# A Fourier mixing and SoLU kernel: the first stage reordered, weight conversion between the folds

## The chip, the cores and the metric

The kernel runs on one core of one Trainium2 chip. The metric is the device time of one execution in microseconds; lower is better. Before the change it was 1299.51 us, the median of three runs (1297.58 to 1300.37).

## The reference

```python
X = np.fft.fft(np.fft.fft(x, axis=1), axis=2).real   # x: (8, 3136, 256)
h = X.reshape(25088, 256) @ w_in                     # w_in: (256, 1024)
e = np.exp(h - h.max(-1, keepdims=True))
solu = h * e / (e.sum(-1, keepdims=True) + 1e-9)
ln = (solu - mean(solu)) / sqrt(var(solu) + 1e-6) * g_ln
out = ln @ w_out                                     # w_out: (1024, 256)
```

The weights arrive as 64-bit floats, x as 32-bit floats; all work is done in 32 bits.

## The kernel before, in words

**The transform.** The sequence of 3136 is split into 49 x 64. The eight sequences are taken in four pairs. For one pair x is read in eight chunks of four columns (`load`: a plain part xa on SP's queue, L98, and a mirrored part xb by an indirect transfer on GpSimd's queue, L100). `add_mirror` (L120, L121, GpSimd) adds the mirrored part, `fold` (L111 to L113, VectorE) folds the 256 features, `transform1` (L151, TensorE) does the 49-point transform of two columns, ScalarE copies the result to z (L154), and SP stores z to the DRAM buffer zd once per chunk (L156). The tiles xa and xb have two buffers, so chunk c + 2 is loaded when chunk c is folded. `turn` (L163, GpSimd's queue) reads zd back in another order, five frequencies at a time, as four transfers into a tile g; `transform2` (L174) does the 64-point transform of one frequency.

**The units.** 25 frequencies for each of four pairs make 100 units. A unit has up to two signs with 128 rows each. Its instructions: `up` (L200, TensorE, product with the prepared w_in), `even` and `join` (L206, L214, VectorE), `expo` (L225, ScalarE), `product` (L233, VectorE, and L235, GpSimd), `square` (L242, ScalarE), the turn of 32 x 32 blocks (L269, VectorE), the move of the turned blocks (L278, SP's queue, 16 transfers for two units), `stats` (L249 to L257, GpSimd). Four units later `down` (L284, TensorE) multiplies with the prepared w_out, ScalarE scales (L289) and the result is stored. While pair p is in its units, the chunks of pair p + 1 are loaded, summed, folded and transformed, one step per unit (`ahead` and `ahead_pe`).

**The first stage.** For pair 0 nothing can run beside the units, so its eight chunks go through `ahead` and `ahead_pe` alone. In the same time ScalarE's queue loads the tables and both weights. Then `prepare` runs: VectorE converts w_in from 64 to 32 bits (`narrow`, L316 to L347, four pieces of 512 columns), TensorE multiplies it with the feature table Q (L379), VectorE converts w_out (eight pieces of 256 columns), scales it by g_ln (L384), and subtracts its column mean (L388 to L391). The scratch pool of this stage is closed before the working pool of the units is opened in its place.

**What sets the order.** The schedule is written by hand: each engine carries out its instructions in the order of the program, and each waits for the data and the buffers it needs. A transfer is issued by the engine whose queue it stands in, in that order.

Of the kernel before, what the change touches and what calls it, by code (L numbers as in the profile page):

```python
# [33 lines left out]
def kernel(  # L34
# [272 lines left out]
    def load_weight(pool, w, o, engine):  # L307

        if w.dtype == FP32:
            engine.dma_start(out=o, in_=w.rearrange("(c p) f -> p c f", p=P))  # L310
            return lambda: None
        raw = pool.tile([P, o.shape[1], 2 * w.shape[1]], I32, name=f"raw_{w.tensor.name}")
        engine.dma_start(out=raw, in_=w.bitcast(I32).rearrange("(c p) f -> p c f", p=P))

        def bits(o, i, a, op0, b=None, op1=ALU.bypass):
            nc.vector.tensor_scalar(out=o, in0=i, scalar1=a, scalar2=b, op0=op0, op1=op1)  # L316

        n = min(w.shape[1], 512)

        def narrow(c, j):  # L320
            def tmp(name, dt=I32):
                return pool.tile([P, n], dt, tag=name, name=name)

            lo, hi = raw[:, c, 2 * j : 2 * (j + n) : 2], raw[:, c, 2 * j + 1 : 2 * (j + n) : 2]

            ex = tmp("ex")
            bits(ex, hi, 20, ALU.logical_shift_right, 0x7FF, ALU.bitwise_and)
            bits(ex, ex, -896.0, ALU.add, 0.0, ALU.max)
            bits(ex, ex, 255.0, ALU.min)
            bits(ex, ex, 23, ALU.logical_shift_left)  # L330

            unit = tmp("unit")
            bits(unit, hi, 31, ALU.logical_shift_right, 31, ALU.logical_shift_left)
            nc.vector.tensor_tensor(out=unit, in0=unit, in1=ex, op=ALU.bitwise_or)  # L334
            top = tmp("top")
            bits(top, hi, 0xFFFFF, ALU.bitwise_and, 3, ALU.logical_shift_left)
            nc.vector.tensor_tensor(out=top, in0=top, in1=unit, op=ALU.bitwise_or)

            half, rest = tmp("ex"), tmp("rest", FP32)
            bits(half, lo, 16, ALU.logical_shift_right, 0xFFFF, ALU.bitwise_and)  # L340
            bits(rest, half, 2.0 ** -36, ALU.mult)
            half = tmp("ex")
            bits(half, lo, 0xFFFF, ALU.bitwise_and)
            nc.vector.scalar_tensor_tensor(out=rest, in0=half, scalar=2.0 ** -52, in1=rest,  # L344
                                           op0=ALU.mult, op1=ALU.add)
            nc.vector.tensor_tensor(out=rest, in0=rest, in1=unit.bitcast(FP32), op=ALU.mult)  # L346
            nc.vector.tensor_tensor(out=o[:, c, j : j + n], in0=rest, in1=top.bitcast(FP32), op=ALU.add)  # L347
# [206 lines left out]
```

## Time and profile before

| | us |
|---|---|
| median of three runs | 1299.51 |
| the profiled execution | 1302.77 |
| its span, first to last instruction | 1301.0 |
| TensorE busy in the span | 1184.9 (91%) |
| VectorE busy | 959.6 (74%) |
| ScalarE busy | 610.2 (47%) |
| GpSimd busy | 554.1 (43%) |

The profile is one execution. Engines: PE is TensorE, PEld its weight loads, DVE is VectorE, ACT is ScalarE, POOL is GpSimd, SP is the engine that issues most transfers; a q behind a name is the engine's sequencer. Starts are in us from the first instruction of the span. In a row, "out<-in" gives the tiles, "x8" the number of instructions merged, and the part in brackets the idle time of the engine ahead of the row and what ended it. PEclk is the clock that TensorE was granted, as a share of 2.4 GHz.

### The profile page before, as it was taken

To read this page: it belongs to the slowest core of one execution; us is meant where nothing else is said; L and a number is where in the kernel's file an instruction comes from. 1 tells how busy PE (TensorE), PEld (TensorE's weight loads), DVE (VectorE), ACT (ScalarE), POOL (GpSimd) and SP (SyncE) were. 2 spreads that over 40 slices of the span, in tenths; PEclk is the share of its full clock that TensorE was granted. 3 is DMA by queue.
4 is the path that set the end of the run, shared out by engine and by line. 5 is a ranking of instruction groups with operands and counts; after the bars stand their busy time and mean duration, and the time that the engine had idled before them with its cause. 6 is when DMAs were issued, how large, how long until landed. Compare 5 with 4: busy or idle time off the path is not lost.

```text
span 1301.0 us, 15863 instructions
## 1 busy us (share of the span) xinstructions
PE 1184.9 (91%) x4864; PEld 899.4 (69%) x4864; DVE 959.6 (74%) x1481; ACT 610.2 (47%) x1149; POOL 554.1 (43%) x972
## 2 busy tenths in 40 slices
PE   1432679999999999999999999999999999999997
PEld 1210347777777777777777777787777777777786
DVE  2399788777777788787777788777777787777770
ACT  1100245545555455555555455555454555555551
POOL 2530245454445355554345445444454333333331
PEclk9656889999999999999999999999999999999999
DMA  9660067886579967665588769675598546454543
GB/s 232 216 152 0 27 132 167 169 164 160 136 146 179 174 149 188 151 165 140 136 172 171 182 146 178 154 169 145 130 172 165 125 111 145 102 133 103 136 106 100
DMA packets 464628, 189.53 MB, mean 146 GB/s; under 512 B 433206, under 2 KB 446782, under 8 KB 464288
## 3 DMA queue, kind: packets, MB, share of 16 engines
q1 hardware_dynamic: 444752, 144.45, 51.1%
q0 software_dynamic: 13824, 38.55, 11.4%
q10 hardware_dynamic: 5968, 5.52, 1.9%
q8 instruction: 40, 0.66, 0.2%
q14 instruction: 44, 0.36, 0.1%
HBM read 44.78 MB, written 38.80 MB: 64 GB/s over the span
## 4 chain that ended last, share of the span: by engine, by line
PE 86%; DVE 8%; DMA 3%; issue 1%; POOL 1%; ACT 0%; POOLq 0%; DVEq 0%; ACTq 0%
PE ps_o L284 52%; PE ps_h L200 25%; PE ps L151 4%; PE ps L174 3%; DMA xa<-in_x_dram 2%; DVE ex L316 2%; DMA xb<-in_x_dram,idx 1%; PE ps L176 1%; POOL xa L120 1%; DVE u L233 1%; DVE h L214 1%; DVE v L269 1%; DVE rest L344 0%; DVE rest L346 0%; DVE unit L334 0%
## 5 line engine op out<-in xcount | busy, mean ns | idle before, releaser
L284 PE MATMUL ps_o<-Wo,uT 128*128 128x256 f32 x3136 | 699.6, 381 | 2.7 <-DMA uT<-v 2.7
L284 PEld LDWEIGHTS ps_o<-Wo,uT 128*128 128x128 f32 x3136 | 613.3, 197 | 65.2 <-issue 3.5
L200 PE MATMUL ps_h<-Wi,q 128*128 128x512 f32 x800 | 363.3, 597 | 13.1 <-DVE ev L206 11.6
L233 DVE SCALAR_TENSOR_TENSOR u<-h,u 128x1024 f32<-128x1024 f32 x196 | 232.5, 1223 | 139.3 <-ACT u L225 139.3
L225 ACT ACTIVATE u<-h,neg 128x1024 f32<-128x1024 f32 x196 | 223.7, 1142 | 200.2 <-DVE neg L219 200.2
L235 POOL TENSOR_SCALAR nmean<-usum 128x1 f32<-128x1 f32 x196 | 127.7, 652 | 433.7 <-DVE u L233 433.4
L242 ACT ACTIVATE h<-u,nmean 128x1024 f32<-128x1024 f32 x196 | 223.6, 1142 | 124.4 <-POOL nmean L235 124.4
L214 DVE CUSTOM_DVE_ANT_0 h<-ev,ps_h 128x1024 f32<-128x1024 f32 x196 | 231.8, 1219 | 48.0 <-PE ps_h L200 44.4
L200 PEld LDWEIGHTS ps_h<-Wi,q 128*128 128x128 f32 x800 | 152.9, 192 | 163.2 <-issue 147.2
L269 DVE STREAM_TRANSPOSE v<-u 128x1024 f32<-128x1024 f32 x200 | 238.1, 1230 | 0.1
L206 DVE SCALAR_TENSOR_TENSOR ev<-w_mid,q,ps_h 128x1024 f32<-128x1024 f32 x100 | 127.6, 1276 | 61.8 <-PE ps_h L200 61.0
L182 ACT COPY q<-ps 128x257 f32<-128x257 f32 x100 | 37.3, 373 | 205.7 <-PE ps L176 203.8
L151 PE MATMUL ps<-y,F 98*100 98x258 f32 (+3 forms) x288 | 81.2, 422 | 47.0 <-DVE y L113 47.0
L296 POOL DMA_INDIRECT out_dram<-ot,idx x96 | 102.6, 1069 | 46.1 <-issue 21.9
L254 POOL TENSOR_SCALAR v<-ssq 128x2 f32<-128x2 f32 (+1 forms) x100 | 27.6, 276 | 170.1 <-ACT h L242 170.1
L289 ACT ACTIVATE ot<-ps_o,rs 128x256 f32<-128x256 f32 x196 | 80.8, 456 | 30.4 <-PE ps_o L284 30.4
L174 PEld LDWEIGHTS ps<-T,g 128*128 128x128 f32 x400 | 60.4, 191 | 47.4 <-issue 47.3
L151 PEld LDWEIGHTS ps<-y,F 98*100 98x100 f32 x288 | 48.4, 192 | 61.0 <-DVE y L113 26.9
L120 POOL TENSOR_TENSOR xa<-xa,xb 98x1020 f32<-98x1020 f32 (+1 forms) x32 | 72.7, 2273 | 29.7 <-DMA xa<-in_x_dram 19.7
L257 POOL TENSOR_TENSOR rs<-v,neg_half 128x2 f32<-128x2 f32 (+1 forms) x100 | 71.9, 719 | 7.8
L174 PE MATMUL ps<-T,g 128*128 128x128 f32 x400 | 60.8, 275 | 0.0
L163 POOL DMA_DIRECT2D g<-zd x80 | 47.5, 604 | 20.6 <-DMA zd<-z 11.3
(53 smaller groups left out, 491.6 us busy)
## 6 DMA issues: line engine op xcount, KB each, us to landing
uT<-v SPq DMA_DIRECT2D x784, 128.0 KB
zd<-z SPq DMA_DIRECT2D x32, 400.0 KB
g<-zd POOLq DMA_DIRECT2D x80, 160.0 KB, 5.3
out_dram<-ot SPq DMA_DIRECT2D x100, 128.0 KB
xa<-in_x_dram SPq DMA_DIRECT2D x32, 392.0 KB
raw_in_moe_w_in_dram<-in_moe_w_in_dram ACTq DMA_DIRECT2D x1, 2048.0 KB
raw_in_moe_w_out_dram<-in_moe_w_out_dram ACTq DMA_DIRECT2D x1, 2048.0 KB
uT<-v SPq DMA_DIRECT2D x32, 64.0 KB
```

Of the source, the lines that this page charges most:

```text
L151: nc.tensor.matmul(o[..., cs], F[:, 2 * t + h, :], i[..., cs], start=first, stop=True, skip_group_check=True)
L174: nc.tensor.matmul(ps[:, h * P : (h + 1) * P], g[:, k, h * P : (h + 1) * P], T[:, k1, :], start=(h == 0), stop=True, skip_group_check=True)
L200: nc.tensor.matmul(ps[:, fs], t.q[:, c * P : (c + 1) * P], Wi[:, c, fs], start=True, stop=True)
L206: nc.vector.scalar_tensor_tensor(out=t.ev, in0=w_mid, scalar=t.q[:, KD * P :], in1=ps, op0=ALU.mult, op1=ALU.add)
L214: nc.vector.tensor_tensor_reduce(out=t.h[s], in0=t.ev, in1=ps, scale=1.0, scalar=-3.0e38, op0=ALU.subtract if s else ALU.add, op1=ALU.max, ...
L225: nc.scalar.activation(out=t.u[s], in_=t.h[s], func=ACT.Exp, bias=t.neg[:, s : s + 1], accum_out=t.esum[:, s : s + 1])
L233: nc.vector.scalar_tensor_tensor(out=t.u[s], in0=t.h[s], scalar=1.0, in1=t.u[s], op0=ALU.mult, op1=ALU.mult, accum_out=t.usum[:, s : s + 1])
L235: nc.gpsimd.tensor_scalar(out=t.nmean[:, s : s + 1], in0=t.usum[:, s : s + 1], scalar1=-1.0 / FF, scalar2=None, op0=ALU.mult)
L242: nc.scalar.activation(out=t.h[s], in_=t.u[s], func=ACT.Square, bias=t.nmean[:, s : s + 1], accum_out=t.ssq[:, s : s + 1])
L269: nc.vector.transpose(out=t.batch.v[:, t.w, :, o], in_=t.u[s])
L284: nc.tensor.matmul(ps, uT[:, c, :, s], Wo[:, c, :], start=(c == 0), stop=(c == KF - 1))
L296: dma = nc.gpsimd.indirect_dma_start(out=out, out_offset=bass.IndirectOffsetOnAxis(ap=idx[:, i : i + 1], axis=0), in_=t.ot[s], in_offset=None)
```

## The change

It concerns the first stage, and what of it is moved behind the first units.

- The working pool `fpool` is opened at the start. Its buffers hold, before the units use them: the raw w_in (tag v), the converted w_in (h), Q (ev), chunks 2 to 5 of x (uT), the raw transform table (v), and later the raw w_out (uT).
- Six chunks of x are loaded at once (two in their own buffers, four in the uT buffers), and chunk c + 6 when chunk c is folded. All weights and tables are now in SP's queue; w_in comes in four pieces between the chunks.
- For pair 0 the mirrored sum is done by VectorE; the other pairs keep GpSimd.
- `narrow` has eight instructions for a piece of 512 columns (for w_out two pieces of 256 together, with g_ln in the last two), where it had 14; two of them work in place on the raw data.
- The four pieces of w_in are converted behind folds 0 to 3; the products with Q stand behind transforms 4 to 6.
- The table T is loaded compactly and put into place by two copies on ScalarE.
- The raw w_out is loaded behind chunk 5, in eight transfers. Half of it is converted behind the last fold, a quarter behind unit 0, a quarter behind unit 1. Its column mean is formed behind unit 2, and subtracted by GpSimd.
- Only the first `turn` of pair 0 stands ahead of the units; the other four follow units 0 to 3.

```diff
--- before.py
+++ after.py
@@ -71,6 +71,7 @@
     small = ctx.enter_context(tc.tile_pool(name="small", bufs=7))
     dram = ctx.enter_context(tc.tile_pool(name="dram", bufs=2, space=bass.MemoryType.DRAM))
     ps_h = ctx.enter_context(tc.tile_pool(name="ps_h", bufs=1, space=PSUM))
+    fpool = ctx.enter_context(tc.tile_pool(name="fpool", bufs=2))
     ps_m = ctx.enter_context(tc.tile_pool(name="ps_m", bufs=4, space=PSUM))
     F = const.tile([PR, 6, ZR], FP32, name="F")
@@ -81,6 +82,9 @@
     neg_half = const.tile([P, 2], FP32, name="neg_half")
     idx = const.tile([P, NP * (NC + NK - 1)], I32, name="idx")
     w_mid = const.tile([P, FF], FP32, name="w_mid")
+    g_ln = const.tile([P, KF], FP32, name="g_ln")
+    wbar = const.tile([P, D], FP32, name="wbar")
+    top_bit = const.tile([P, 1], I32, name="top_bit")
@@ -90,11 +94,14 @@
             self.raw, self.y, self.y0 = {}, {}, None
             self.g = {}
-    def load(pr, c):
+    def load(pr, c, room=None):
         r = slice(pr.p * PR, (pr.p + 1) * PR)
-        xa = xpool.tile([PR, CH, D], FP32, tag="xa", name="xa")
-        xb = xpool.tile([PR, CH, D], FP32, tag="xb", name="xb")
+        if room is None:
+            xa = xpool.tile([PR, CH, D], FP32, tag="xa", name="xa")
+            xb = xpool.tile([PR, CH, D], FP32, tag="xb", name="xb")
+        else:
+            xa, xb = (t.rearrange("p (l d) -> p l d", d=D) for t in room)
         nc.sync.dma_start(out=xa, in_=x_pn[r, c * CH + 1 : (c + 1) * CH + 1, :])
         i = pr.p * NC + c
         nc.gpsimd.indirect_dma_start(
@@ -112,13 +119,13 @@
         nc.vector.tensor_tensor(out=o[:, :, 129:256], in0=up, in1=down, op=ALU.subtract)
         nc.vector.tensor_copy(out=o[:, :, 0:129:128], in_=i[:, :, 0:129:128])
-    def add_mirror(pr, c):
+    def add_mirror(pr, c, engine):
         xa, xb, _ = pr.raw[c]
         n = CH - 1 if c == NC - 1 else CH
         a, rb = xa[:, 0:n, :], xb[:, ::-1, :][:, 0:n, :]
-        nc.gpsimd.tensor_tensor(out=a[:, :, 1:D], in0=a[:, :, 1:D], in1=rb[:, :, D - 1 : 0 : -1], op=ALU.add)
-        nc.gpsimd.tensor_tensor(out=a[:, :, 0:1], in0=a[:, :, 0:1], in1=rb[:, :, 0:1], op=ALU.add)
+        engine.tensor_tensor(out=a[:, :, 1:D], in0=a[:, :, 1:D], in1=rb[:, :, D - 1 : 0 : -1], op=ALU.add)
+        engine.tensor_tensor(out=a[:, :, 0:1], in0=a[:, :, 0:1], in1=rb[:, :, 0:1], op=ALU.add)
     def fold(pr, c):
@@ -304,92 +311,118 @@
-    def load_weight(pool, w, o, engine):
+    NW = 512
+    tmp = const.tile([P, NW], I32, name="tmp")
+    def load_piece(w, raw, o, c, j, n):
         if w.dtype == FP32:
-            engine.dma_start(out=o, in_=w.rearrange("(c p) f -> p c f", p=P))
...
+            nc.sync.dma_start(out=o[:, j : j + n], in_=w.rearrange("(c p) f -> p c f", p=P)[:, c, j : j + n])
+        else:
+            src = w.bitcast(I32).rearrange("(c p) f -> p c f", p=P)
+            nc.sync.dma_start(out=raw, in_=src[:, c, 2 * j : 2 * (j + n)])
+    def bits(o, i, a, op0, b=None, op1=ALU.bypass):
+        nc.vector.tensor_scalar(out=o, in0=i, scalar1=a, scalar2=b, op0=op0, op1=op1)
+    def narrow(w, raw, outs):
+        if w.dtype == FP32:
+            for o, scale in outs:
+                nc.vector.tensor_scalar(out=o, in0=o, scalar1=scale, scalar2=2.0 ** 20, op0=ALU.mult, op1=ALU.mult)
+            return
+        lo, hi, unit = raw[:, 0 : 2 * NW : 2], raw[:, 1 : 2 * NW : 2], tmp
+        bits(unit, hi, 20, ALU.logical_shift_right, 0x7FF, ALU.bitwise_and)
+        bits(unit, unit, -896.0, ALU.add, 0.0, ALU.max)
+        bits(unit, unit, 255.0, ALU.min, 2.0 ** 23, ALU.mult)
+        nc.vector.scalar_tensor_tensor(out=unit, in0=hi, scalar=top_bit, in1=unit, op0=ALU.bitwise_and,
+                                       op1=ALU.bitwise_or)
+        bits(hi, hi, 0xFFFFF, ALU.bitwise_and, 0x100000, ALU.bitwise_or)
+        bits(lo, lo, 1, ALU.logical_shift_right)
+        m = lo.bitcast(FP32)
+        nc.vector.scalar_tensor_tensor(out=m, in0=lo, scalar=2.0 ** -31, in1=hi, op0=ALU.mult, op1=ALU.add)
+        n = NW // len(outs)
+        for i, (o, scale) in enumerate(outs):
+            r = slice(i * n, (i + 1) * n)
+            nc.vector.scalar_tensor_tensor(out=o, in0=m[:, r], scalar=scale, in1=unit[:, r].bitcast(FP32),
+                                           op0=ALU.mult, op1=ALU.mult)
+    class Weights:
+        def load_in(self):
+            raw = fpool.tile([P, 2, FF, 2], FP32, tag="v", name="raw_in", bufs=2)
+            raw = raw.rearrange("p a f b -> p (a f b)").bitcast(I32)
+            self.w_in = [fpool.tile([P, FF], FP32, tag="h", name="w_in", bufs=2) for _ in range(KD)]
+            self.pieces = []
             for c in range(KD):
-                nc.vector.tensor_scalar(out=mid[:, c, :], in0=ones, scalar1=Q[:, c, D:], scalar2=None, op0=ALU.mult)
-            for h in range(KD + 1):
-                ps = ps_h.tile([P, FF], FP32, tag=f"h{h % 2}", name="wps")
-                for half in range(2):
-                    fs = slice(half * HW, (half + 1) * HW)
-                    for c in range(KD):
-                        lhsT = mid[:, c, :] if h == KD else Q[:, c, h * P : (h + 1) * P]
-                        nc.tensor.matmul(ps[:, fs], lhsT, w_in[:, c, fs], start=(c == 0), stop=(c == KD - 1))
-                nc.scalar.copy(w_mid if h == KD else Wi[:, h, :], ps)
-
-            narrow_out()
+                for j in range(0, FF, NW):
+                    i = 2 * (c * FF + j)
+                    self.pieces.append((moe_w_in, raw[:, i : i + 2 * NW], self.w_in[c], c, j, NW))
+        def piece_in(self, i):
+            load_piece(*self.pieces[i])
+        def narrow_in(self, i):
+            w, raw, o, c, j, n = self.pieces[i]
+            narrow(w, raw, [(o[:, j : j + n], 2.0 ** -20)])
+        def load_tables(self):
+            self.Q = fpool.tile([P, KD, D + 1], FP32, tag="ev", name="Q", bufs=1)
+            nc.sync.dma_start(out=self.Q, in_=q_tab.rearrange("(c p) d -> p c d", p=P))
+            nc.sync.dma_start(out=g_ln, in_=moe_g_ln.rearrange("(c p) -> p c", p=P))
+        def load_table(self):
+            self.T = fpool.tile([P, NK, N2], FP32, tag="v", name="T_raw", bufs=2)
+            for b in range(2):
+                nc.sync.dma_start(out=self.T[b * N2 : (b + 1) * N2], in_=t_tab)
+        def place_table(self):
+            for b in range(2):
+                r = slice(b * N2, (b + 1) * N2)
+                nc.scalar.copy(T[r, :, r], self.T[r])
+        def mid(self):
+            self.m = w_mid[:, 0 : KD * P].rearrange("p (c k) -> p c k", c=KD)
+            for c in range(KD):
+                nc.vector.tensor_scalar(out=self.m[:, c, :], in0=ones, scalar1=self.Q[:, c, D:], scalar2=None,
+                                        op0=ALU.mult)
+        def product_in(self, h):
+            ps = ps_h.tile([P, FF], FP32, tag=f"h{h % 2}", name="wps")
+            for half in range(2):
+                fs = slice(half * HW, (half + 1) * HW)
+                for c in range(KD):
+                    lhsT = self.m[:, c, :] if h == KD else self.Q[:, c, h * P : (h + 1) * P]
+                    nc.tensor.matmul(ps[:, fs], lhsT, self.w_in[c][:, fs], start=(c == 0), stop=(c == KD - 1))
+            nc.scalar.copy(w_mid if h == KD else Wi[:, h, :], ps)
+        def load_out(self):
+            raw = fpool.tile([P, 2, KF, 4, 64], FP32, tag="uT", name="raw_out", bufs=2)
+            self.raw = raw.rearrange("p w c i m -> p (w c i m)").bitcast(I32)
             for c in range(KF):
-                nc.vector.tensor_scalar(out=Wo[:, c, :], in0=Wo[:, c, :], scalar1=g_ln[:, c : c + 1],
-                                        scalar2=None, op0=ALU.mult)
+                load_piece(moe_w_out, self.raw[:, 2 * c * D : 2 * (c + 1) * D], Wo[:, c], c, 0, D)
+            nc.vector.tensor_scalar(out=g_ln, in0=g_ln, scalar1=2.0 ** -20, scalar2=None, op0=ALU.mult)
+        def narrow_out(self, i):
+            m = NW // D
+            narrow(moe_w_out, self.raw[:, 2 * i * NW : 2 * (i + 1) * NW],
+                   [(Wo[:, c], g_ln[:, c : c + 1]) for c in range(i * m, (i + 1) * m)])
+        def centre(self):
             cs = ps_m.tile([P, D], FP32, tag="m", name="cs")
             for c in range(KF):
                 nc.tensor.matmul(cs, ones, Wo[:, c, :], start=(c == 0), stop=(c == KF - 1))
             nc.scalar.mul(out=wbar, in_=cs, mul=1.0 / FF)
             for c in range(KF):
-                nc.vector.tensor_tensor(out=Wo[:, c, :], in0=Wo[:, c, :], in1=wbar, op=ALU.subtract)
-        return prepare
+                nc.gpsimd.tensor_tensor(out=Wo[:, c, :], in0=Wo[:, c, :], in1=wbar, op=ALU.subtract)
@@ -401,7 +434,7 @@
             load(pr, 1)
         elif 0 <= c < NC:
             if r == 0:
-                add_mirror(pr, c)
+                add_mirror(pr, c, nc.gpsimd)
             else:
                 fold(pr, c)
                 if c + 2 < NC:
@@ -416,19 +449,49 @@
     with tc.manual_schedule():
         pairs = [Pair(p) for p in range(NP)]
+        first, weights = pairs[0], Weights()
         nc.sync.dma_start(out=idx, in_=mirror)
-        nc.scalar.dma_start(out=F, in_=f_tab)
-        ahead(pairs[0], 0)
+        rooms = {}
+        for c in range(2, 6, 2):
+            room = fpool.tile([P, 2, KF, 4, 64], FP32, tag="uT", name="room", bufs=2)
+            room = room[0:PR].rearrange("p w c i m -> p (w c i m)").rearrange("p (a n) -> p a n", a=4)
+            rooms[c], rooms[c + 1] = [room[:, i] for i in (0, 1)], [room[:, i] for i in (2, 3)]
+        load(first, 0)
+        nc.sync.dma_start(out=F, in_=f_tab)
+        weights.load_in()
+        weights.piece_in(0)
+        for c in range(1, 4):
+            load(first, c, rooms.get(c))
+            weights.piece_in(c)
+        weights.load_tables()
+        for c in range(4, 6):
+            load(first, c, rooms[c])
         nc.vector.memset(ones, 1.0)
         nc.vector.memset(neg_half, -0.5)
+        bits(top_bit, neg_half[:, 0:1].bitcast(I32), 31, ALU.logical_shift_right, 31, ALU.logical_shift_left)
         nc.vector.memset(T, 0.0)
-        with tc.tile_pool(name="prep", bufs=1) as prep:
-            prepare = load_weights(prep)
-            for step in range(1, NK):
-                ahead(pairs[0], step)
-                ahead_pe(pairs[0], step)
-            prepare()
-        fpool = ctx.enter_context(tc.tile_pool(name="fpool", bufs=2))
+        for c in range(NC):
+            add_mirror(first, c, nc.vector)
+            fold(first, c)
+            if c + 6 < NC:
+                load(first, c + 6)
+            for s in range(CH // 2):
+                transform1(first, c * CH // 2 + s)
+            if c < 4:
+                weights.narrow_in(c)
+            if c == 2:
+                weights.load_table()
+            elif c == 3:
+                weights.mid()
+            elif 3 < c < 7:
+                weights.product_in(c - 4)
+            if c == 5:
+                weights.load_out()
+        weights.place_table()
+        turn(first, 0)
+        for i in range(2):
+            weights.narrow_out(i)
         units = [Unit(p, k1) for p in range(NP) for k1 in range(NK)]
         units[0].q = take2(transform2(pairs[0], 0))
@@ -470,6 +533,12 @@
                 elif cur.w:
                     move_blocks(batch, slice(0, 2))
                 stats(cur)
+            if i < 2:
+                weights.narrow_out(i + 2)
+            elif i == 2:
+                weights.centre()
+            if 0 < i + 1 < NK // KG:
+                turn(first, i + 1)
             if ahd:
                 ahead(ahd, cur.k1)
             if old and 1 in old.signs:
```

## Rows read from the trace of the kernel before

**Rows 1.** The page's chain of work that ended last: shares of the span by engine.

```profile
PE 86%; DVE 8%; DMA 3%; issue 1%; POOL 1%; ACT 0%; POOLq 0%; DVEq 0%; ACTq 0%
```

**Rows 2.** Busy time by stage (stretch, its us, each engine's busy us, PEclk, DMA share, GB/s).

```profile
0.00:65.50 65.50, 22.73 (x57) 14.22 (x58) 19.91 (x30) 9.30 (x15) 28.38 (x28) 0.79 0.84 223
65.50:95.36 29.86, 9.89 (x22) 4.96 (x21) 28.49 (x59) 1.17 (x2) 11.93 (x20) 0.56 0.69 164
95.36:133.76 38.40, 10.12 (x18) 4.13 (x18) 35.65 (x116) 3.04 (x3) 0.00 (x0) 0.63 0.00 1
133.76:183.76 50.00, 32.30 (x97) 18.89 (x98) 39.51 (x66) 18.89 (x35) 16.31 (x32) 0.88 0.26 64
183.76:1257.20 1073.44, 1073.44 (x4514) 825.10 (x4513) 828.78 (x1206) 568.51 (x1076) 489.07 (x880) 1.00 0.69 152
```

**Rows 3.** The chain in order of time, first 184 us (start, us, what).

```profile
3.87 12.30 DMA xb<-in_x_dram,idx
19.90 2.68 DVE y L113
33.99 2.34 POOL xa L120
54.36 7.40 DMA xa<-in_x_dram
```

**Rows 4.** Groups by shape, VectorE, first 145 us; the last from the page.

```profile
L316 DVE TENSOR_SCALAR ex<-raw_in_moe_w_in_dram 128x512 int32<-128x512 int32 x12 | 5.3, 444 | 0.1
L344 DVE SCALAR_TENSOR_TENSOR rest<-ex,rest 128x512 f32<-128x512 int32 x4 | 2.8, 692 | 0.1
L344 DVE SCALAR_TENSOR_TENSOR rest<-ex,rest 128x256 f32<-128x256 int32 x8 | 3.4, 426 | 0.3
L111 DVE TENSOR_TENSOR y<-xa 98x508 f32<-98x508 f32 x8 | 5.5, 688 | 44.1 <-POOL xa L120 44.1
L233 DVE SCALAR_TENSOR_TENSOR u<-h,u 128x1024 f32<-128x1024 f32 x196 | 232.5, 1223 | 139.3 <-ACT u L225 139.3
```

**Rows 5.** Timeline and tile g: the last copy of z to the first unit.

```profile
69.57 0.58 ACT L154 COPY z<-ps 100x512 f32<-100x512 f32 x1 [1.63 <-PE ps L151]
75.17 5.94 POOL L163 DMA_DIRECT2D g<-zd  x10 [11.29 <-DMA zd<-z]
DMA to landing us min/median/max: 4.4/5.3/5.3
139.28 0.61 PE L174 MATMUL ps<-T,g 128*128 128x128 f32 x4
142.82 1.28 DVE L206 SCALAR_TENSOR_TENSOR ev<-w_mid,q,ps_h 128x1024 f32<-128x1024 f32 x1 [0.15 <-DVE Wo L391]
```

**Rows 6.** Timeline of TensorE: products with w_in, 512 columns each.

```profile
88.21 3.78 PE L379 MATMUL wps<-w_in,Q 128*128 128x512 f32 x4 [13.20 <-DVE w_in L347]
95.49 6.69 PE L379 MATMUL wps<-w_in,Q 128*128 128x512 f32 x10 [3.50 <-DVE w_in L347]
102.02 3.60 PE L379 MATMUL wps<-w_in,w_mid 128*128 128x512 f32 x8
```

**Rows 7.** Busy time 30 to 65.5 us, and all transfers up to 75.2 us.

```profile
30.00:65.50 35.50, 16.33 (x41) 9.99 (x42) 11.56 (x21) 5.68 (x10) 18.86 (x16) 0.62 0.70 218
DMA packets 9148, 15.86 MB, mean 211 GB/s; under 512 B 4804, under 2 KB 5286, under 8 KB 8891
```

**Rows 8.** GpSimd: issues of g by form; pair 1's first mirrored sum.

```profile
L163 POOL DMA_DIRECT2D g<-zd x60 | 35.6, 605 | 8.4 <-issue 8.3
172.02 2.35 POOL L120 TENSOR_TENSOR xa<-xa,xb 98x1020 f32<-98x1020 f32 x1
```

**Rows 9.** Timeline: unit 3's turn of blocks, pair 1's first transform.

```profile
178.06 2.37 DVE L269 STREAM_TRANSPOSE v<-u 128x1024 f32<-128x1024 f32 x2
181.74 2.02 PE L151 MATMUL ps<-y,F 98*100 98x258 f32 x4 [4.18 <-DVE y L113]
```

**Rows 10.** SP's queue: one batch of moved blocks.

```profile
201.72 15.07 SPq L278 DMA_DIRECT2D uT<-v  x16
```

More of the change, by code (lines that the diff above doesn't have):

```diff
@@ L303, in store @@
             tc.add_to_no_dep_group(f"out{s}", dma.ins)
-    def load_weight(pool, w, o, engine):
+    NW = 512
+    tmp = const.tile([P, NW], I32, name="tmp")
+    def load_piece(w, raw, o, c, j, n):
         if w.dtype == FP32:
-            engine.dma_start(out=o, in_=w.rearrange("(c p) f -> p c f", p=P))
[L311 to L347, printed above, removed]
-        def run():
-            for c in range(o.shape[1]):
-                for j in range(0, w.shape[1], n):
-                    narrow(c, j)
-        return run
@@ L355, in load_weights @@
-    def load_weights(pool):
-        w_in = pool.tile([P, KD, FF], FP32, name="w_in")
-        g_ln = pool.tile([P, KF], FP32, name="g_ln")
-        Q = pool.tile([P, KD, D + 1], FP32, name="Q")
-        mid = w_mid[:, 0 : KD * P].rearrange("p (c k) -> p c k", c=KD)
-        wbar = pool.tile([P, D], FP32, name="wbar")
-        narrow_in = load_weight(pool, moe_w_in, w_in, nc.scalar)
-        nc.scalar.dma_start(out=Q, in_=q_tab.rearrange("(c p) d -> p c d", p=P))
-        nc.scalar.dma_start(out=g_ln, in_=moe_g_ln.rearrange("(c p) -> p c", p=P))
-        for b in range(2):
-            nc.scalar.dma_start(out=T[b * N2 : (b + 1) * N2, :, b * N2 : (b + 1) * N2], in_=t_tab)
-        narrow_out = load_weight(pool, moe_w_out, Wo, nc.scalar)
-        def prepare():
-            narrow_in()
-            for c in range(KD):
-                nc.vector.tensor_scalar(out=mid[:, c, :], in0=ones, scalar1=Q[:, c, D:], scalar2=None, op0=ALU.mult)
-            for h in range(KD + 1):
-                ps = ps_h.tile([P, FF], FP32, tag=f"h{h % 2}", name="wps")
-                for half in range(2):
-                    fs = slice(half * HW, (half + 1) * HW)
-                    for c in range(KD):
-                        lhsT = mid[:, c, :] if h == KD else Q[:, c, h * P : (h + 1) * P]
-                        nc.tensor.matmul(ps[:, fs], lhsT, w_in[:, c, fs], start=(c == 0), stop=(c == KD - 1))
-                nc.scalar.copy(w_mid if h == KD else Wi[:, h, :], ps)
-            narrow_out()
-            for c in range(KF):
-                nc.vector.tensor_scalar(out=Wo[:, c, :], in0=Wo[:, c, :], scalar1=g_ln[:, c : c + 1],
-                                        scalar2=None, op0=ALU.mult)
```

## The prediction

> **What bounds the kernel now.** I read the stages first. The shares of the chain show TensorE with 86% of the span, VectorE with 8%, transfers with 3% [rows 1]. The table by stage says where the rest lies: from 183.76 us to 1257.20 us TensorE is busy for 1073.44 of 1073.44 us at granted clock 1.00. Before that come four stages where it isn't: 65.50 us of folds, 29.86 us converting w_in, 38.40 us converting w_out (VectorE busy 35.65 of them, transfers at zero), and 50.00 us of first units, in which VectorE leads [rows 2]. The reader is to see one thing: a microsecond won before 183.76 us comes off the end, as the work of TensorE behind it doesn't change. So the question is when the 183.76 us point falls now. I build the new first stage on the span's clock.
>
> The chain, in order of time, shows what the folds wait for: 12.30 us for the first mirrored chunk, later 7.40 us for chunk 7, whose buffer comes free late; and two column copies of 2.68 us, held up beside the sums on GpSimd [rows 3]. Six chunks under way and sums on VectorE remove both kinds; the next thing to be late is VectorE itself.
>
> **First data.** Two queues instead of three now feed the first chunk, with w_in's first piece behind it. Bounds: 3.87 + 12.30 = 16.2 us as now, and 3.87 + 4.4 = 8.3 us, if it lands like the fastest transfer from DRAM shown [rows 3, 5]. I take 12.0. The loads issued behind it have 7 us of VectorE work per chunk as cover, so I cost them at nothing; without the cover that is the transfer rival below.
>
> **VectorE up to the last fold.** The sum of 1020 elements isn't there on VectorE; its nearest row is the 1024-wide product, 1.223 us, against 2.34 on GpSimd [rows 3, 4]. A chunk is then 1.22 + two halves of 0.69 [rows 4] + two short ones, 0.2 each: 3.0 us, eight make 24.0. A piece of w_in goes from 14 instructions to eight: five 512-wide TENSOR_SCALAR at 0.444 and three two-input ones at 0.692 [rows 4] = 4.3 us; four make 17.2 instead of 29.86. Two of the five now also write with a stride of two: between 0.444, the row that reads with that stride and is the nearest, and 0.692; I take 0.444, and keep 0.25 x 2 a piece for the range. The mean vector and chunk 7's extra fold add 0.6 + 0.7. The last fold ends at 12.0 + 24.0 + 17.2 + 0.6 + 0.7 = 54.5 us.
>
> **TensorE beside it.** The three products with w_in are put between the transforms of chunks 4 to 7. Fold 4 ends at 12.0 + 5 x 3.0 + 17.2 + 0.6 = 44.8. From there TensorE has 12 matmuls of 512 columns and four transforms of eight 256-column ones, 28 wide ones in all. One costs 0.945 us at the lower clock (1.2 GHz), 0.45 at the full (2.4 GHz), and 0.669 in a stretch of ten that began low and ended high [rows 6]. Bounds: 28 x 0.45 = 12.6, so 57.4 us; 28 x 0.945 = 26.5, so 71.3. I take ten at 0.669 and 18 at 0.45 = 14.8: 59.6 us, later than VectorE's own end. With the copy of z, 0.58 [rows 5], the last store of z is issued at 60.2.
>
> **Stores, turn, first unit.** Now the last copy ends at 69.57 + 0.58 = 70.15 and GpSimd is released at 75.17: 5.0 us for a store with little beside it [rows 5]. In the change, the eight loads of w_out stand in SP's queue ahead of the stores of chunks 6 and 7, and turn waits for those. They are issued when chunk 5's store is: TensorE has 12 wide matmuls up to there, 10 x 0.669 + 2 x 0.45 = 7.6 behind 44.8, and the copy, so 53.0; 2.1 MB + two stores of 0.41 MB at 218 GB/s [rows 7] last 13.4 us, so 66.4 instead of 60.2 + 5.0 = 65.2. Turn is four issues at 0.605 [rows 8], the last landing 4.4 to 5.3 us later [rows 5]: 66.4 + 2.4 + 4.8 = 73.6. From transform2 to the first ev is 142.82 - 139.28 = 3.5 us [rows 5]: 77.1 against 142.82, a gain of 65.7. T's compact load and its two copies into place (1600 columns, 1.8 us each by the z copy) lie on ScalarE in the 13 us between 60.2 and 73.6. VectorE converts half of w_out there: a 1024-word round is 5 x 0.444 + 2 x 0.692 + 2 x 0.426 [rows 4] = 4.46 us, two end near 54.5 + 1.5 (wait for the data) + 8.9 = 65, with 12 us to spare. Turns 1 to 4 now stand behind units 0 to 3 on GpSimd, 2.4 us each; behind 0 and 1 its idle time covers them (busy 16.31 of 50.00 us [rows 2]). That w_in's pieces and the tables move from ScalarE's queue to SP's puts nothing in front of chunk 0 and 1.2 us of transfer (0.24 MB of F) before the first piece of w_in.
>
> **First units.** The two other rounds stand in VectorE's order behind units 0 and 1. Its idle time there is a wait for the exponential inside a unit, which cannot hold them: +8.9. The column sums for the mean of w_out run on TensorE, which is busy for 32.30 of 50.00 us in the stage of first units [rows 2], in its wait for unit 2's ev: nothing; in full they would be 16 half-wide matmuls, 3.6 us at 0.45 a wide one. The subtractions go to GpSimd behind unit 2: eight of 256 columns. A row of 1020 takes 2.35 [rows 8], so 0.59 each by proportion, 2.35 at most if it doesn't shrink; I take 0.7, 5.6 us. Behind them stand a turn, 2.4, and pair 1's first mirrored sum, which now starts at 172.02 [rows 8]; it would end at 172.02 + 8.0 + 2.55 = 182.6 on the old clock. VectorE wants it when unit 3's blocks are turned, at 178.06 + 2.37 = 180.4 [rows 9]: +2.2 (bounds 0 and 15). TensorE waits for that fold now too, 4.18 us before 181.74 [rows 9], so it counts in full.
>
> The Trainium skill (GPSIMD Engine Reference, Key points) says that GpSimd shares its SBUF interfaces with VectorE and is disturbed by instructions with two SBUF inputs. Here the sum at 172.02 ran beside such ones in 2.35 us, the one at 33.99 beside an idle VectorE in 2.34, so the trace doesn't show it; by the rule the eight subtractions would each wait for an instruction of VectorE, which is the fourth rival.
>
> **Sum.** -65.7 + 8.9 + 2.2 = -54.6. The profiled execution took 1302.77 us, 1.77 beyond its span of 1301.0; against it that is 1248.2. It lies 3.26 above the median of the runs, 1299.51; from the median: 1244.9, so 1245.
>
> **Rivals.** (1) TensorE stays at the lower clock through chunks 4 to 7: 71.3 instead of 59.6, +11.7 less 1.2 us (the stores no longer queue behind w_out): 1255.5. For: 0.62 to 0.79 was granted in the first stage [rows 2, 7]; against: the dense stretch of ten rose. 14%. (2) Transfers bound the stage: 15.06 MB are needed up to the last store of z (15.86 moved by 75.2 us, less two loads of pair 1) [rows 7]; at 218 GB/s that is 69.1 us, plus one to start: 70 instead of 66.4, 1249. For: the engines' share is 0.84 over the first 65.50 us [rows 2]; against: T's 256-byte rows, which stood in that share, are gone. 8%. (3) It doesn't do what it says, since a conversion waits for the whole tile, not its piece: w_in's fourth piece and all queued before it are 6.4 MB, 28.7 us at 223 GB/s [rows 2], where fold 0 ends at 15: +13.7, 1259. Against: product matmuls already run at 88.21, while the conversion of the same tile goes on to 95.36 [rows 2, 6]. 6%. (4) GpSimd late in unit 3: subtractions at 2.35 each make 18.8 instead of 5.6, +13.2: 1258. 6%. (5) All bounds good: first data at 8.3, TensorE at full clock, no queueing, no GpSimd wait: -3.7 - 2.2 - 1.2 - 2.2, with chunks of 2.8 us -1.6: 1234. 10%. (6) Slower than before: the working pool is now opened ahead of the first stage, so its tiles lie at other addresses. If the moves of turned blocks became slower by it, SP would bind the long stage: 16 moves occupy SP for 15.07 us [rows 10] of the 22.6 that two units last (1073.44 us for 95 units, rows 2). It begins to cost at 1.5 times the present length, and takes the gain at 1.58 (1.2 us in each of 48 pairs); at 1.75 it is 3.8 x 48 - 55 = 127 us slower: 1427. Against: sizes, shapes and order of these moves are unchanged. 4%.
>
> **Numbers.** The forecast has 50%, with 1236 to 1254 as its own range; 2% are left for no effect. What this kernel's runs can tell from no change is about 0.2%, 2.6 us. The range 1230 to 1262 takes in rivals 1 to 5 and leaves out the slower one and pile-ups of two bad bounds. Faster 94%, same 2%, slower 4%.
>
> **What would show it.** First ev at about 77 us; last fold near 54.5; the last transform at 59 to 60 with the clock rising in it; turn released near 66; units 0 and 1 longer by 4.5 us each; the fold of pair 1 waiting some 2 us for GpSimd; the long stage unchanged at 1073 us. It is wrong if VectorE waits for transfers between chunks 1 and 7, if one conversion takes over 5 us, or if the long stage grows.

## The result, and the profile after

The changed kernel took 1255.93 us, the median of four runs (1255.59 to 1256.66); the kernel before, timed beside it, 1299.94. The ratio is 0.9665 [0.9648, 0.9681]: 3.35% faster, and 11 us over the 1245 forecast. The profiled execution took 1256.66 us with a span of 1254.8; its gain against that of before is 46.1 us, where the working gave 54.6.

The stages of the changed kernel, cut where its chain changes hands, against [rows 2]:

```profile
43.97:64.99 21.02, 21.02 (x64) 12.16 (x64) 11.94 (x28) 7.12 (x11) 0.00 (x0) 0.85 0.63 199
64.99:77.41 12.42, 0.01 (x1) 0.04 (x1) 4.65 (x10) 3.53 (x3) 2.42 (x4) 0.60 0.59 178
77.41:137.11 59.70, 35.96 (x97) 19.89 (x98) 44.86 (x67) 18.78 (x35) 28.06 (x49) 0.79 0.46 91
137.11:1211.00 1073.89, 1073.89 (x4514) 824.74 (x4514) 828.90 (x1207) 568.83 (x1076) 494.22 (x888) 1.00 0.71 152
```

The long stage is the same (1073.89 against 1073.44 us, clock 1.00), so the whole gain lies ahead of it: it begins at 137.11 instead of 183.76 us, 46.65 earlier. And the first row shows where the forecast fell short: from 43.97 to 64.99, for 21.02 us, TensorE is busy without a gap, at a granted clock of 0.85; the working gave this stretch 14.8 us.

Its chain in order of time (start, us, what), which answers [rows 3]:

```profile
2.85 10.30 DMA xb<-in_x_dram,idx
43.97 3.70 PE ps L158 x8
47.68 4.80 PE wps L403 x8
66.03 6.02 DMA xa<-in_x_dram
74.12 3.15 DMA g<-zd
79.28 6.26 PE ps_h L207 x8
```

First data cost 10.30 us instead of 12.30. Between 54 and 66 us the chain of the view passes through a fold, a load of w_out and its conversion. The piece at 66.03 is a load of x in the same queue that landed when turn was released; in the program turn waits for the stores of z ahead of it, and in experiments 4 and 10 the view names the store. The last of these was issued near 65.6, behind ScalarE's last copy of z, which waited for TensorE:

```profile
65.03 0.59 ACT L161 COPY z<-ps 100x512 f32<-100x512 f32 x1 [0.68 <-PE ps L158]
```

So I read TensorE's stretch as what sets turn, and experiment 2 tests it. Then the timeline of TensorE, against [rows 5] and [rows 6]:

```profile
43.97 3.70 PE L158 MATMUL ps<-y,F 98*100 98x258 f32 x8 [3.58 <-DVE y L120]
47.47 5.01 PE L403 MATMUL wps<-w_in,Q 128*128 128x512 f32 x8
52.32 1.89 PE L158 MATMUL ps<-y,F 98*100 98x258 f32 x8
54.05 3.60 PE L403 MATMUL wps<-w_in,Q 128*128 128x512 f32 x8
57.48 1.89 PE L158 MATMUL ps<-y,F 98*100 98x258 f32 x8
59.21 3.60 PE L403 MATMUL wps<-w_in,w_mid 128*128 128x512 f32 x8
62.65 2.34 PE L158 MATMUL ps<-y,F 98*100 98x258 f32 x16
77.41 1.19 PE L181 MATMUL ps<-T,g 128*128 128x128 f32 x4 [12.42 <-DMA g<-zd]
79.28 6.25 PE L207 MATMUL ps_h<-Wi,q 128*128 128x512 f32 x8 [0.47 <-ACT q L189]
```

Each product with w_in is x8, so three are 24 rows of 512 columns, not 12. Behind 12.42 us without work the product of unit 0 took 6.25 us at a granted clock of 0.59; the same eight in unit 1 (at 86.55) took 3.70 at 1.00. VectorE and GpSimd of the same execution, in two views, against [rows 4, 5, 8, 9]:

```profile
13.18 1.22 DVE L127 TENSOR_TENSOR xa<-xa,xb 98x1020 f32<-98x1020 f32 x1 [8.64 <-DMA xb<-in_x_dram,idx]
54.25 0.69 DVE L118 TENSOR_TENSOR y<-xa 98x508 f32<-98x508 f32 x1 [4.23 <-PE ps L158]
60.68 0.43 DVE L329 TENSOR_SCALAR tmp<-raw_out 128x512 int32<-128x512 int32 x1 [4.59 <-DMA raw_out<-in_moe_w_out_dram]
83.17 1.28 DVE L213 SCALAR_TENSOR_TENSOR ev<-w_mid,q,ps_h 128x1024 f32<-128x1024 f32 x1 [13.28 <-PE ps_h L207]
96.38 1.28 DVE L213 SCALAR_TENSOR_TENSOR ev<-w_mid,q,ps_h 128x1024 f32<-128x1024 f32 x1
110.77 1.27 DVE L213 SCALAR_TENSOR_TENSOR ev<-w_mid,q,ps_h 128x1024 f32<-128x1024 f32 x1
126.58 1.75 DVE L240 SCALAR_TENSOR_TENSOR u<-h,u 128x1024 f32<-128x1024 f32 x1 [1.37 <-ACT u L232]
133.64 0.69 DVE L118 TENSOR_TENSOR y<-xa 98x508 f32<-98x508 f32 x1 [1.36 <-POOL xa L127]
```

```profile
72.28 2.42 POOL L170 DMA_DIRECT2D g<-zd  x4 [49.44 <-DMA xa<-in_x_dram]
122.40 6.51 POOL L425 TENSOR_TENSOR Wo<-Wo,wbar 128x256 f32<-128x256 f32 x8
131.25 2.36 POOL L127 TENSOR_TENSOR xa<-xa,xb 98x1020 f32<-98x1020 f32 x1
```

VectorE itself has 13.28 us without work ahead of unit 0, which the second half of w_out could have filled, and chunk 7's fold waited 4.23 us for a transform to free one of the two y buffers.

### The profile page after: what moved, and what is told of

Its sections match the earlier page's. It is cut to its first block, busy times and chain, and to the rows that moved or that the text cites. A ratio compares the mean times of both kernels' runs of the same rounds, so it can differ in the third digit from the quotient of the medians.

```text
span 1254.8 us, 15771 instructions
## 1 busy us (share of the span) xinstructions
PE 1181.9 (94%) x4864; PEld 897.2 (72%) x4864; DVE 930.4 (74%) x1383; ACT 613.0 (49%) x1151; POOL 541.5 (43%) x964
## 4 chain that ended last, share of the span: by engine, by line
PE 89%; DVE 5%; DMA 2%; issue 1%; POOL 1%; ACT 1%; POOLq 0%; DVEq 0%; ACTq 0%; SPq 0%
PE ps_o L291 54%; PE ps_h L207 26%; PE ps L158 4%; PE ps L181 3%; PE ps L183 1%; DMA xb<-in_x_dram,idx 1%; DVE tmp L329 1%; POOL Wo L425 1%; DMA xa<-in_x_dram 0%; DVE h L221 0%; DVE tmp L342 0%; DVE u L240 0%; DMA raw_out<-in_moe_w_out_dram 0%; PE wps L403 0%; DVE y L119 0%
## 5 line engine op out<-in xcount | busy, mean ns | idle before, releaser
L207 PE MATMUL ps_h<-Wi,q 128*128 128x512 f32 x800 | 367.5, 603 | 12.7 <-DVE ev L213 11.8
L240 DVE SCALAR_TENSOR_TENSOR u<-h,u 128x1024 f32<-128x1024 f32 x196 | 233.6, 1228 | 140.0 <-ACT u L232 140.0
L161 ACT COPY z<-ps 100x512 f32<-100x512 f32 x64 | 36.2, 569 | 41.8 <-PE ps L158 26.8
```

What stands on the lines that cost most here:

```text
L207: nc.tensor.matmul(ps[:, fs], t.q[:, c * P : (c + 1) * P], Wi[:, c, fs], start=True, stop=True)
L240: nc.vector.scalar_tensor_tensor(out=t.u[s], in0=t.h[s], scalar=1.0, in1=t.u[s], op0=ALU.mult, op1=ALU.mult, accum_out=t.usum[:, s : s + 1])
```

## The experiments

Diffs are cut to the lines that matter; they are against the changed kernel, the first against the kernel before, and where a heading says "as 2" or names other edits, on top of those. Ratios are to the kernel before, about 1300 us each time.

**1. The short conversion alone.** The eight-instruction `narrow` in the old place and order.

```diff
-        n = min(w.shape[1], 512)   # narrow: 14 instructions a piece
+        NW = 512                   # narrow: the eight of the changed kernel
-            narrow_out()           # then eight products with g_ln
+            narrow_out(g_ln)       # g_ln in the last two
```

> The kernel before, in its old order, with the shorter conversion alone (eight instructions for 512 columns, two rounds of 256 for w_out with g_ln inside). Theory A, most of the gain is the shorter conversion: w_in's four pieces take 17.4 us instead of 29.9 and w_out's four rounds 18.3 instead of 38.4 plus 2.2 of scaling; both stood bare on the chain, so 30 to 34 us of the 44 come here: 1266 to 1270. Theory B, the gain is the new order: the conversion's share is hidden again by the wait for the turned tiles and the products with w_in, under 22 us come here: above 1278.

1265.0 us, 0.9725 [0.9709, 0.9741]. The shorter conversion gives 35 of the 44 us; with it in place, the whole new order adds 9. VectorE converts w_in in 17.8 us instead of 29.9, and w_out with its scaling in 18.6 instead of 40.2: 33.7 us saved where the conversions stand alone on VectorE, and about as much gained.

**2. The products behind the transforms.**

```diff
-            elif 3 < c < 7:
-                weights.product_in(c - 4)
+        for h in range(KD + 1):     # behind the loop over chunks
+            weights.product_in(h)
```

> The changed kernel with the three products with w_in moved from behind transforms 4 to 6 to behind transform 7. Theory A, TensorE sets the end of the first stage from 44 to 65 us, because each product is eight matmuls in the trace and not four: the last z is stored 7 to 9 us sooner, the products fill the 12.4 us in which TensorE waits for the turned tile, and unit 0 starts on a warm clock (3 us): 8 to 12 us gained, 1244 to 1248. Theory B, the transfers (w_out ahead of the last two stores) set it: the stores land when they did, gain only the 3 us of the clock, 1253.

1251.67 us, 0.9630 [0.9614, 0.9647]: 4.3 us better, between the two. Its TensorE, and turn on GpSimd:

```profile
44.24 10.75 PE L158 MATMUL ps<-y,F 98*100 98x258 f32 x40 [3.58 <-DVE y L120]
54.83 7.03 PE L403 MATMUL wps<-w_in,Q 128*128 128x512 f32 x16
72.40 1.19 PE L181 MATMUL ps<-T,g 128*128 128x128 f32 x4 [7.11 <-DMA g<-zd]
```

```profile
67.28 2.41 POOL L170 DMA_DIRECT2D g<-zd  x4 [44.17 <-DMA xa<-in_x_dram]
```

The transforms end at 54.99 instead of 64.99, and the last store is issued at 59.0 instead of 65.6. So the products stood in the way. But turn is released at 67.28, only 5.0 earlier: in SP's queue the eight loads of w_out (52.14 to 58.44) now stand ahead of the last stores, the queueing that the prediction had priced at 1.2 us.

**3. All of w_out converted ahead of unit 0.**

```diff
-        for i in range(2):
+        for i in range(4):
             weights.narrow_out(i)
-            if i < 2:
-                weights.narrow_out(i + 2)
```

> The changed kernel with all four rounds of w_out converted ahead of unit 0, instead of two there and two behind units 0 and 1. Theory A, the two rounds behind the units are bare and cost 4.5 us each, while VectorE idles from 69.9 us to the first ev at about 82: 9 us gained, 1247. Theory B, the idle time is needed or the conversion disturbs the issue of the turn on GpSimd: under 4 us, above 1252.

1248.99 us, 0.9605 [0.9589, 0.9621]: 6.9 us better. Its ev rows:

```profile
83.75 1.28 DVE L213 SCALAR_TENSOR_TENSOR ev<-w_mid,q,ps_h 128x1024 f32<-128x1024 f32 x1 [3.53 <-PE ps_h L207]
92.57 1.25 DVE L213 SCALAR_TENSOR_TENSOR ev<-w_mid,q,ps_h 128x1024 f32<-128x1024 f32 x1
102.43 1.24 DVE L213 SCALAR_TENSOR_TENSOR ev<-w_mid,q,ps_h 128x1024 f32<-128x1024 f32 x1
```

The first ev comes no sooner, but the units behind it are 8.82 and 9.86 us apart instead of 13.21 and 14.39: 8.9 us fewer, of which the median shows 6.9. The two rounds end at 80.2, inside VectorE's wait.

**4. Mirrored sums of pair 0 on GpSimd, as before.**

```diff
-            add_mirror(first, c, nc.vector)
+            add_mirror(first, c, nc.gpsimd)
```

> The changed kernel with pair 0's mirrored sums back on GpSimd. Theory A, two engines share the work but VectorE's one-input instructions wait for the sum that runs beside them, as the column copies did before (2.7 instead of 0.3 us): 3 to 8 us lost, 1259 to 1264. Theory B, only VectorE's own time counts: 1.3 us less per chunk up to fold 4, 3 us gained, 1253.

1266.97 us, 0.9749 [0.9733, 0.9766]: 11.0 us worse, more than either theory, and no better than experiment 1. TensorE's stretch begins at 55.25 instead of 43.97, which is about the whole loss: the first piece of w_in took VectorE 10.9 us and the third 12.1, instead of 4.4 and 4.3. The timeline of both engines:

```profile
22.30 3.07 DVE L329 TENSOR_SCALAR raw_in<-raw_in 128x512 int32<-128x512 int32 x2
22.38 2.35 POOL L127 TENSOR_TENSOR room<-room 98x1020 f32<-98x1020 f32 x1
25.30 2.34 POOL L127 TENSOR_TENSOR room<-room 98x1020 f32<-98x1020 f32 x1 [0.21 <-DMA room<-in_x_dram]
25.41 2.79 DVE L348 SCALAR_TENSOR_TENSOR raw_in<-raw_in 128x512 f32<-128x512 int32 x1
```

Beside a sum on GpSimd, L348 takes 2.79 us where it takes 0.69 alone, and the two of L329, which have one input, 3.07 where they take 0.76. L348 ends at 28.20, 0.56 us behind the end of the sum (27.64), as if it had waited for it. GpSimd's own sums of 1020 stay at 2.34 to 2.52; only its short ones of four columns go from 0.20 to as much as 0.66. The order pays only with GpSimd silent while VectorE converts. The Trainium skill (GPSIMD Engine Reference, Key points) says that GpSimd shares its SBUF interfaces with VectorE and contends with its instructions that have two SBUF inputs or run in a two-port mode. For L348, which has two, the trace agrees (2.79 against 0.69 us), and it adds which side loses and how much; in which mode L329 runs, no view shows.

**5. As 2, with the loads of w_out behind the last store.**

```diff
-            if c == 5:
-                weights.load_out()
+        weights.load_out()          # behind the products
```

> The kernel of the second experiment (products late) with the loads of w_out moved in SP's queue from behind the store of chunk 5 to behind the last store of z. Theory A, with the products out of the way the eight loads of w_out hold up the last two stores: there the last store was issued at 59 us and the turn released only at 67.3; now it is released 3 to 5 us sooner, near 63, and unit 0 starts 3 to 4 us sooner, which leaves 1247 to 1249 against 1251.7. Theory B, a store takes 8 us whatever stands ahead of it: no change or, since w_out comes late for its conversion, 1252 to 1256.

1253.99 us, 0.9640 [0.9625, 0.9655]: 2.3 us above 2, though the runs overlap (1251.69 to 1255.51, and 1250.40 to 1253.20 there). Turn is released at 64.03, 3.2 sooner than in 2, so the loads had held the stores. The tile g, though (TensorE's timeline, then the view of g):

```profile
76.10 1.20 PE L181 MATMUL ps<-T,g 128*128 128x128 f32 x4 [10.62 <-DMA g<-zd]
```

```profile
DMA to landing us min/median/max: 8.5/9.8/10.4
```

Its four transfers take 8.5 to 10.4 us instead of 3.0, beside 2.1 MB of w_out. The cost of these bytes moved; it didn't go.

**6. As 3, with the column mean behind unit 1.**

```diff
-            if i == 2:
+            if i == 1:
                 weights.centre()
```

> The kernel of the third experiment (w_out converted ahead of unit 0) with the column mean formed and subtracted behind unit 1 instead of unit 2. Theory A, the subtractions on GpSimd (6.5 us) and the turn of the tiles held up pair 1's first mirrored sum behind unit 2, and behind unit 1 no such sum stands: 2 to 3 us gained, 1246 to 1247 against 1249.0. Theory B, they hold up unit 2's means instead: no gain.

1249.01 us, 0.9610 [0.9595, 0.9625]: nothing against 3. The subtractions, a unit earlier, now slow unit 2: its ev and the next are 11.47 us apart, 10.07 in experiment 3. And pair 1's first mirrored sum, which no longer waits for them, now runs beside unit 3's `product` (L240), which takes 1.23 alone:

```profile
117.01 3.67 DVE L240 SCALAR_TENSOR_TENSOR u<-h,u 128x1024 f32<-128x1024 f32 x1 [1.37 <-ACT u L232]
```

**7. TensorE kept busy in its wait.** Twelve products, 24 rows, whose result nobody reads, ahead of turn.

```diff
+        warm = ps_m.tile([P, HW], FP32, tag="m", name="warm")
+        for _ in range(12):
+            nc.tensor.matmul(warm, ones, Wi[:, 0, 0:HW], start=True, stop=True)
         turn(first, 0)
```

> The changed kernel with 12 more matmuls of 512 columns (24 in the trace), whose result nobody reads, on TensorE between the last transform and the first turned tile. Theory A, unit 0 is 3 us late because TensorE's clock falls to 1.2 GHz in the 12.4 us of that wait: its eight product matmuls take 3.7 instead of 6.25 us, 2 to 3 us gained, 1253 to 1254. Theory B, the clock is not what delays unit 0: no change, 1256, or later if the extra matmuls outlast the wait.

```profile
63.65 10.46 PE L494 MATMUL warm<-Wi,ones 128*128 128x512 f32 x24
75.64 0.68 PE L181 MATMUL ps<-T,g 128*128 128x128 f32 x4 [1.53 <-DMA g<-zd]
76.91 3.70 PE L207 MATMUL ps_h<-Wi,q 128*128 128x512 f32 x8 [0.46 <-ACT q L189]
```

Unit 0's product is back at 3.70 us, and from transform2 to the join it is 5.0 instead of 8.15: the slow start, 3.1 us, is a matter of the clock after idleness (granted 1.00 over these eight, 0.59 in the changed kernel). Unit 0 also began 1.8 us sooner, which the edit doesn't explain. In the whole it can't be told: 1255.49 us (1254.28 to 1259.72), 0.9666 [0.9651, 0.9681]. In the profiled execution the long stage begins 4.9 us sooner and the span is 2.4 shorter: 1.2 us is lost within the long stage, and 1.3 at its end, where TensorE's wait ahead of the last `down` grows from 2.87 to 4.18.

**8. All together, w_out's loads split around the stores.** Edits 2, 3 and 6; the first half of w_out behind chunk 3, the second behind the last store.

```diff
-            if c == 5:
+            if c == 3:
                 weights.load_out()              # now c = 0 to 3 only
+        weights.rest_out(KF // 2, KF)           # behind the products
```

> Products with w_in behind transform 7, all of w_out converted ahead of unit 0, its mean behind unit 1, and its loads split: the first half behind chunk 3, the second behind the last store. Theory A, the gains add since each stands at its own place: last z stored at about 57, turn released near 62, first ev near 72 instead of 82, units 0 and 1 each 4.5 us shorter, no wait for GpSimd: 20 to 23 us gained on the changed kernel, 1233 to 1236. Theory B, the conversion of w_out becomes the bound ahead of unit 0, as its data come late: VectorE ends it at 75 to 80, which leaves 12 to 18 us: 1238 to 1244.

1247.27 us, 0.9593 [0.9576, 0.9610]: 8.7 us better, not 20. Turn is released at 64.36, but its tile lands at 74.18, beside the second half of w_out: what 5 showed.

**9. Edits 2 and 3, all loads of w_out behind chunk 3.**

```diff
-            if c == 5:
+            if c == 3:
                 weights.load_out()
```

> As the third and second experiments together (products late, all of w_out converted ahead of unit 0, its mean behind unit 2), with all eight loads of w_out issued behind chunk 3, so that neither the last stores nor the turned tile queue behind them. Theory A, w_out's 2.1 MB are what the kernel with its loads split still paid for (there the turned tile landed 7.3 us after its last issue instead of 3.2): the turn is released at 62 to 64, the first ev is near 73 to 75, and 16 to 19 us are gained on the changed kernel: 1237 to 1240. Theory B, the stores of chunks 4 and 5 then queue behind them and hold up the copies of z: the last store comes 4 us or more later, 1243 to 1247.

1243.09 us (1242.33 to 1244.66), 0.9564 [0.9548, 0.9580]: with experiment 11 the fastest of all, 12.8 us under the changed kernel and 1% faster than it.

```profile
54.97 7.03 PE L403 MATMUL wps<-w_in,Q 128*128 128x512 f32 x16
72.92 1.19 PE L181 MATMUL ps<-T,g 128*128 128x128 f32 x4 [7.48 <-DMA g<-zd]
74.79 5.35 PE L207 MATMUL ps_h<-Wi,q 128*128 128x512 f32 x8 [0.46 <-ACT q L189]
```

```profile
122.53:1197.00 1074.47, 1074.47 (x4514) 825.12 (x4513) 829.07 (x1206) 568.72 (x1077) 492.61 (x888) 1.00 0.71 152
```

The long stage begins at 122.53, 14.6 us sooner than in the changed kernel. Less came than hoped because the stores of z now follow w_out: a copy of z waits 5.72 us for one, and turn is released at 67.60, no sooner than in 2. Unit 0 still starts at a lower clock, 0.69. What the early loads gave is not shown: 2 and 3 gained 4.3 and 6.9 us, 11.2 together, and the two edits were not run together with the loads left behind chunk 5.

**10. Two chunks under way instead of six.**

```diff
-            if c + 6 < NC:
-                load(first, c + 6)
+            if c + 2 < NC:
+                load(first, c + 2)
```

> The changed kernel with two chunks of x under way instead of six (chunk c + 2 is loaded when chunk c is folded, all in the own buffers of x). Theory A, conversions between folds 0 to 3 already cover a load of 7 us, and from chunk 4 on TensorE's queue does: under 4 us lost, below 1260. Theory B, chunks 4 to 7 come 7 us apart as they did before, since VectorE needs only 2.6 us for one: 10 to 17 us lost, 1266 to 1273.

1256.51 us, 0.9668 [0.9651, 0.9684]: no difference. VectorE does wait for chunks (2.32, 0.72 and 4.21 us), but TensorE ends its transforms at 65.6, 65.0 with six, though the first chunk came 1.4 us later here: the waits fit behind the matmuls. Nor were six ever under way in the changed kernel. Its timeline of SP has the plain part of the fifth chunk at issue for 15.78 us:

```profile
10.85 15.78 SPq L105 DMA_DIRECT2D room<-in_x_dram  x1
```

The sixth follows at 26.69, and the first store of z, in the same queue, at 28.77 (21.81 with two chunks). What held this issue no run shows; the stretch from 43.97 on did not wait for it.

**11. As 9, with GpSimd's order changed:** the mirrored sum ahead of the subtractions, two turns later.

```diff
-            if 0 < i + 1 < NK // KG:
+            if i in (0, 1):
                 turn(first, i + 1)
+            if i == 2:              # behind the ahead step
+                weights.centre()
+            if i in (5, 7):
+                turn(first, (i + 1) // 2)
```

> As the kernel with early loads of w_out (products late, all of w_out converted ahead), with pair 1's first mirrored sum put ahead of the subtractions behind unit 2, and turns 3 and 4 of pair 0 behind units 5 and 7 instead of 2 and 3. Theory A, behind unit 2 it is the order on GpSimd that makes VectorE's fold wait: 1.5 to 3 us gained on that kernel. Theory B, the subtractions slow VectorE's two-input instructions wherever they stand (1.75 instead of 1.23 us beside them): under 1 us.

1243.71 us, 0.9568 [0.9552, 0.9584]: nothing. The first transform of pair 1 runs at 120.67 instead of 120.71: where the sum no longer waits, VectorE is slowed by the subtractions in another place (L240 takes 3.27 and 1.73 us beside them).

## Why the prediction was right, and where it failed

The direction and the mechanism held: the folds and conversions shrank and the long stage kept its length. The time lies within the range of 1230 to 1262, which was wide enough for the rivals, and outside the forecast's own 1236 to 1254. The gain was 8.5 us short on the profiled executions. By the points of the prediction:

| step | forecast | measured | late by |
|---|---|---|---|
| first ev of unit 0 | 77.1 | 83.17 | 6.1 |
| units 0 and 1, longer by | 8.9 | 9.98 | 1.1 |
| GpSimd behind unit 2 | +2.2 | +3.0 | 0.8 |
| long stage, longer by | 0 | 0.45 | 0.5 |

**First data** came at 13.18, not 12.0, and VectorE made it up with chunks of 2.6 us instead of 3.0; a piece of w_in took 4.36 (4.3 forecast), and the writes with a stride of two cost nothing extra: 0.425 us each, 0.444 taken. Fold 4 ended at 43.83 (44.8). Here the working was right.

**TensorE beside it** is the step that failed, in one term. It said "12 matmuls of 512 columns"; there are 24, since each product with w_in shows as eight rows. The 12 that were missed are 12 x 0.45 = 5.4 us, and the last transform ended at 64.99 instead of 59.6: 5.4 later. That the two agree so well is in part chance: the stretch was 6.2 us longer and began 0.8 sooner, and its start at the low clock (3.70 and 5.01 us for rows that later took 1.89 and 3.60) cost 3.2 us where the forecast had 2.2. [Rows 6] had the count: they are 4 + 10 + 8 = 22 rows of one pass of products, and the same timeline has the other two, where I reckoned from the program's lines:

```profile
72.93 2.08 PE L379 MATMUL wps<-w_in,Q 128*128 128x512 f32 x2 [3.39 <-DVE w_in L347]
```

Experiment 2 shows that this term stood on the path, and that 1.2 us for the loads queued ahead of the stores was too little once TensorE was out of the way (3.2 by experiment 5). Rival 1, the low clock, came within half a microsecond of the measured time by luck: the granted clock was 0.62 up to 52.3 us and 1.00 behind it, so the clock did rise.

**Turn and unit 0.** From the last copy of z (65.62) to turn's release it took 6.7 us (6.2 forecast), from there to the tile 5.1 instead of 7.2, which hid 2.1 us of the loss. Then the first ev came 5.8 us behind transform2, not 3.5, and the join another 0.9 late: 3.2 us of the low clock after 12.42 us without work, which I had not foreseen and experiment 7 removed from unit 0. I took the 3.5 from [rows 5], where TensorE had run shortly before. The second wait was there to be seen in my own working: TensorE free from 59.6 to 73.6.

**Units 0 and 1.** The two rounds cost 4.5 us each as forecast (the second 4.54), the clock the rest. Experiment 3 shows that they needn't have stood there.

**GpSimd.** The eight subtractions took 6.51 (5.6 forecast), 0.81 each, and the fold waited 1.36 for the sum (2.2 forecast). Half of the 3.0 us is something else: beside the subtractions VectorE's L240 took 1.75 and 1.73 where it takes 1.23, and L226 0.65 instead of 0.17, 1.5 us together. I had read from the sum at 172.02 that the trace shows no disturbance by instructions with two inputs in SBUF. That reading was wrong: beside it ran `join`, whose second input ps_h lies in PSUM, the memory that TensorE writes to:

```profile
171.80 1.22 DVE L214 CUSTOM_DVE_ANT_0 h<-ev,ps_h 128x1024 f32<-128x1024 f32 x1 [0.17 <-DVE ev L206]
```

And I looked at the wrong engine: GpSimd nearly keeps its speed, and VectorE loses, by a factor of four for L348 in experiment 4. The column copies of 2.68 us in [rows 3] showed it already. Whether the subtractions would cost less on VectorE, where they took 2.77 us before, was not run.

**Rivals.** Transfers as the bound of the folds: not so, since VectorE waits for no chunk behind the first (13.18), and two chunks under way are as fast. A conversion that waits for the whole tile: not so, the first piece follows its fold at 15.71. Subtractions at 2.35 each: not so, 0.81. Slower moves of blocks: not so, the long stage kept its length. So of the three edits in the first stage, chunks under way are worth nothing measurable, sums on VectorE 11 us with the rest in place, the short conversion 35 alone; these are differences in one order of edits each, and need not add up.

**Still open** is why turn is released 5.5 to 8.3 us after the last store is issued (experiments 10 and 2), against 5.0 before: stores that compete with loads, or the stores' own delay. Taking the loads of w_out away from ahead of them brought it from 8.3 to 6.1 (experiment 5); no run parted the rest.

## What to carry to other kernels

Count instructions from the rows of the profile, not from the lines of the program, before multiplying by a duration. When one stage is packed tighter, list what each engine does in the wait that remains: here it held work for VectorE worth 7 us. Bytes that are needed late cost something on either side of a store that is waited for: just ahead of it they held it up by 3.2 us, just behind it they slowed the transfer that reads it back. Loaded early, they stood in the fastest kernel, but no run shows what that alone gained.

## What the runs showed of the hardware

Beside a GpSimd sum of 98 x 1020, VectorE's 512-column instructions took as much as 2.73 us with one input (0.43 alone) and 2.79 with two (0.69 alone), while the sum stayed at 2.34 to 2.52 (experiment 4). Behind 12.42 us without matmuls TensorE did eight of 512 columns in 6.25 us at a granted clock of 0.59, behind 7.11 us (experiment 2) in 5.48 at 0.67, behind 1.53 us (experiment 7) in 3.70 at 1.00. VectorE's in-place instructions with a stride of two took 0.425 us for 512 columns, plain ones 0.427. Transfers of g of 3.0 to 3.3 us in experiment 2 took 8.5 to 10.4 beside 2.1 MB of loads in experiment 5.
